# One instruction stream, two orders: attention and channel mixing with tables derived under a GpSimd and VectorE exclusion

## The chip, the cores and the metric

The kernel runs on one core of a Trainium2 chip. A core has engines that work side by side, each on its own list of instructions and in the order of that list: TensorE (PE in the profile; PEld is its loading of weights) multiplies matrices into PSUM, VectorE (DVE) and ScalarE (ACT) work element by element and over rows, GpSimd (POOL) does element-wise work from and to SBUF, and SyncE (SP) issues transfers. The metric is the device time of one execution in microseconds (us), lower is better.

## The reference

```
kv_pool = kv.reshape(B, H//4, 4, W//4, 4, C).mean(axis=(2, 4))     # 768 keys per batch
k = v = kv_pool.reshape(B, -1, C) @ w_sr
s = (q @ k.T) / sqrt(C);  s -= s.max(-1);  a = exp(s);  a /= a.sum(-1) + 1e-9
x = a @ v                                                          # 4 batches, 12288 rows, 128 channels
x_prev = x shifted down by one row (zero at the top)
xk = mu_k * x + (1 - mu_k) * x_prev;   xr = mu_r * x + (1 - mu_r) * x_prev
h = relu(xk @ w_k)**2                                              # 1024 hidden channels
out = sigmoid(xr @ w_r) * (h @ w_v)
```

## The kernel before

A tile is 512 rows of one batch, so there are 24 tiles a batch and 96 in all. The products run in 16-bit halves: an operand is split into a rounded part and a rest (a name that ends in `h` and one in `l`), and TensorE multiplies the pairs that matter. One tile goes through these steps; the name of a step in the tables stands first, the tile or buffer that the profile shows in brackets.

- `qf` loads the queries, `qh` (ACT) rounds them, `ql` (POOL) takes the rest.
- For each of 4 groups of 128 rows, s = 0 to 3: `S` (PE) the scores against 768 keys, `nm` (DVE) their negative maximum, `ex` (ACT) the exponential (`pe`; for the fourth group it is written back into `S`), `rc` (DVE) the reciprocal of the sums, `f1` (ACT) and `f2` (DVE) the two halves of the normalised weights (`pp<-pe` from SBUF, `pp<-S` from PSUM for the fourth group), `tt` (SP) their transposing transfer (`pT`).
- `AV0` to `AV5` (PE) the sums over the keys (`px`); `xek` and `xer` (ACT) scaled copies for the shift; `xk`, `xr` (DVE) the mixed rows; `xkh`, `xrh` (DVE) and `xkl`, `xrl` (POOL) their halves.
- For each of 4 pairs of hidden blocks, f = 0 to 3: `ha`, `hb` (PE, `ph`), `r` (ACT, `rr`) the positive part, `k2` the square in 32 bits (`kk`; DVE for f = 0 and 1, ACT for 2, and for 3 on DVE back into `ph`), `kh` its rounded half (ACT; DVE for f = 2), `kl` the rest (POOL; DVE for f = 3), `va`, `vb` (PE, `pv`) the second product.
- `z` (PE, `pz`), `E` and `th` (ACT), `E1`, `T1`, `g` (DVE) the gate, `o` (DVE) the output, `so` (SP) its store.

Beside the tiles, `batch_prep` prepares the keys of the next batch: `L_kv` and `br` load and pool them piece by piece over 12 tiles, `pk` and `ks` project them, `am` and `ex` find a scale, `ksh` (a 512-column and a 256-column piece), `kb`, `kd` make the score operands (`ksh`, `kbl`), `vh`, `vl` (`vv`) and `tv` (`vT`) the value operand, `dg`, `dm`, `xt`, `sv`, `uz` the constants of the gate. The weights are prepared once at the start (`w..._wk0` and the like).

What sets the order is a table. Every step is put into a heap under a number, and the heap is emptied from the smallest on; each engine keeps the order in which its instructions were given:

```
if i < len(EARLY):
    places, base = EARLY[i], 0.0
elif i >= NTILES - len(LATE):
    places, base = LATE[i - (NTILES - len(LATE))], i * PERIOD
else:
    places, base = WHEN, i * PERIOD
```

So the first 8 tiles have a table each (`EARLY`), the last 4 too (`LATE`), and the 84 between share one (`WHEN`), shifted by `PERIOD` = 19.3 a tile; `PREP` and `SUM` place the preparation of the next batch in the same way, `ONCE` the weights and the first batch's keys. The numbers only rank; no step waits for a clock. A buffer is taken from its ring when the step that fills it is given: three PSUM buffers serve `S` and `ph` in turn, one serves `px`, `pz` and `pk`, one `pv`. Thus the order also says which step must have read a buffer before another may fill it: `ha0` waits for the fourth `kl` of the tile ahead, `ha1` for the third `ex`, `ha2` for the fourth `f2`, `ha3` for `r2`, the first `S` for `k20`, the second for `k21`, the third for the first `ex`, the fourth for the second. All steps go through one helper, so that nearly all rows of the profile have its line, L39; they are told apart by the names of their tiles.

Of the kernel before, what the change touches and what calls it, by code (L numbers as in the profile page):

```python
# [73 lines left out]
def tile_kernel(ctx, tc, qT, kv0a, kv0b, kvw, head, w_k, w_v, w_r, outT):  # L74
# [712 lines left out]
    for i, (b, t) in enumerate(seq):  # L787
# [44 lines left out]
    "L": 45.13984, "br": 55.31514,  # L832
# [53 lines left out]
    },  # L886
    {
# [268 lines left out]
```

## Time and profile before

| | |
|---|---|
| median of 3 runs | 1902.59 us (1902.36 to 1903.91) |
| profiled execution | 1902.11 us, its span 1900.3 us |
| TensorE | 1844.3 us busy, 97% of the span, 8837 matmuls |
| VectorE | 1750.9 us, 92%, 2400 instructions |
| ScalarE | 1690.0 us, 89%, 2430 |
| GpSimd | 1110.4 us, 58%, 793 |

The busy time of TensorE is modelled (its matmuls are pipelined), so idle time in it says more than busy time. A row of a time line reads: start and length in us, engine, line, operation, what is written from what, its shape, and in brackets the idle time of the engine before it with what ended it. In a row by tiles the three numbers are the shortest, median and longest duration in ns.

### The profile page before, as it was taken

What the parts mean: (1) busy time and instruction counts of PE and PEld (TensorE: products, weight loads), DVE (VectorE), ACT (ScalarE), POOL (GpSimd) and SP (SyncE); (2) the same over time, 40 slices, a digit from 0 to 9 for tenths busy, and PEclk for the clock granted to TensorE, in tenths of its full rate; (3) what the DMA queues carried; (4) which work ended last, traced back from release to release, by engine and by line L of the source; (5) the groups of instructions that cost most, each with busy time, mean ns of one, the idle gap of its engine ahead of it and who ended that gap; (6) DMA issues with size and microseconds to landing.
All of it is one profiled execution on the core that took longest, in us unless ns stands there. A gap on an engine that the chain in (4) does not pass through costs nothing. (4 is left out here: it accounts for less than half of the span.)

```text
span 1900.3 us, 26528 instructions
## 1 busy us (share of the span) xinstructions
PE 1844.3 (97%) x8837; PEld 925.9 (49%) x8983; DVE 1750.9 (92%) x2400; ACT 1690.0 (89%) x2430; POOL 1110.4 (58%) x793
## 2 busy tenths in 40 slices
PE   6899999999999999999999999999999999999999
PEld 3344455445454545445555555544545454545454
DVE  8999999999999999999999999999998989899997
ACT  4788899889999999989999999988999999999997
POOL 2455566566556666556656666656655555555555
PEclk9999999999999999999999999999999999999999
DMA  7655655545465656455556665545645454545462
GB/s 231 136 117 129 147 137 120 106 107 124 99 145 130 148 131 146 96 113 117 119 113 140 139 138 140 130 97 110 120 107 117 107 116 108 115 109 108 91 126 56
DMA packets 643945, 232.12 MB, mean 122 GB/s; under 512 B 612320, under 2 KB 612576, under 8 KB 643808
## 3 DMA queue, kind: packets, MB, share of 16 engines
q1 hardware_dynamic: 643808, 230.43, 54.8%
q8 instruction: 70, 1.15, 0.2%
q14 instruction: 67, 0.55, 0.1%
HBM read 52.63 MB, written 25.17 MB: 41 GB/s over the span
## 5 line engine op out<-in xcount | busy, mean ns | idle before, releaser
L39 POOL TENSOR_TENSOR kl<-kk,kh 128x1024 bf16<-128x1024 f32 x288 | 685.3, 2380 | 182.4 <-ACT kh L39 119.9
L39 ACT ACTIVATE rr<-ph 128x1024 f32<-128x1024 f32 x384 | 392.0, 1021 | 19.3 <-PE ph L39 5.3
L39 PE MATMUL px<-pT,vT 128*128 128x512 f16 x1728 | 391.9, 379 | 2.3 <-DMA pT<-pp 2.2
L39 DVE TENSOR_REDUCE nm<-S 128x1 f32<-128x768 f32 x384 | 360.9, 952 | 27.5 <-PE S L39 22.1
L39 POOL TENSOR_TENSOR xkl<-xk,xkh 128x512 f16<-128x512 f32 x96 | 145.3, 1514 | 320.8 <-DVE xkh L39 318.1
L39 PE MATMUL ph<-xkh,wkl 128*128 128x512 f16 x768 | 293.2, 382 | 15.6 <-DVE pp L39 6.4
L39 ACT ACTIVATE kh<-rr 128x1024 f16<-128x1024 f32 x288 | 304.9, 1059 | 1.5 <-PE pv L39 0.7
L39 DVE SCALAR_TENSOR_TENSOR pp<-pe,rc,pp 128x768 f16<-128x768 f32 x288 | 300.3, 1045 | 0.0
L39 PE MATMUL ph<-xkh,wkh 128*128 128x512 f16 x768 | 292.4, 381 | 0.0
L39 PE MATMUL pv<-kh,wvl 128*128 128x512 f16 x768 | 292.0, 380 | 0.1
L39 PE MATMUL pv<-kh,wvh 128*128 128x512 f16 x768 | 291.1, 379 | 0.0
L39 ACT ACTIVATE pp<-pe,rc 128x768 f16<-128x768 f32 x288 | 267.7, 933 | 4.8 <-DVE rc L39 2.6
L39 ACT ACTIVATE pe<-S,nm 128x768 f32<-128x768 f32 x288 | 262.7, 912 | 8.7 <-DVE nm L39 8.7
L39 PE MATMUL S<-ksh,qh 128*128 128x512 f32 (+1 forms) x768 | 269.4, 432 | 0.0
L39 PEld LDWEIGHTS <-vT 128*128 128x128 f16 x1728 | 168.7, 98 | 206.1 <-issue 3.6
L39 PE MATMUL S<-kbl,qh 128*128 128x256 bf16 (+1 forms) x768 | 251.2, 327 | 2.7
L39 POOL TENSOR_TENSOR xrl<-xr,xrh 128x512 f16<-128x512 f32 x96 | 113.5, 1183 | 239.0 <-DVE xrh L39 239.0
L39 PEld LDWEIGHTS <-wkh 128*128 128x128 f16 x1536 | 150.6, 98 | 180.3 <-issue 12.6
L39 DVE TENSOR_TENSOR kk<-ph,rr 128x1024 f32<-128x1024 f32 x192 | 232.5, 1212 | 2.4 <-ACT rr L39 2.1
L39 PE MATMUL S<-kbl,ql 128*128 128x256 bf16 (+1 forms) x717 | 215.1, 325 | 14.3 <-DVE pp L39 5.3
L39 PE MATMUL ph<-xkl,wkh 128*128 128x512 f16 x768 | 228.2, 379 | 0.0
L39 PE MATMUL pv<-kl,wvb 128*128 128x512 bf16 x673 | 187.1, 379 | 4.7
(119 smaller groups left out, 2655.5 us busy)
## 6 DMA issues: line engine op xcount, KB each, us to landing
qf<-qT SPq DMA_DIRECT2D x96, 256.0 KB, 2.7
outT<-o SPq DMA_DIRECT2D x96, 256.0 KB, 2.7
kvt<-kvw SPq DMA_DIRECT2D x36, 512.0 KB, 3.7
pT<-pp SPq DMA_TRANSPOSE x384, 3.9
kva<-kv0a SPq DMA_DIRECT2D x8, 512.0 KB, 9.8
kvb<-kv0b SPq DMA_DIRECT2D x4, 512.0 KB, 6.4
land<-moe_w_k SPq DMA_DIRECT2D x2, 512.0 KB, 5.4
land<-moe_w_v SPq DMA_DIRECT2D x2, 512.0 KB, 9.7
```

The source lines that it names most:

```text
L39: return self.tc.keep_in_program_order(op(*args, **kwargs))
```

## The change

All numbers of the tables `WHEN`, `PREP`, `SUM`, `ONCE`, `EARLY` and `LATE` are others; the code, `PERIOD`, the rings and the split of the work over the engines are the same. The new tables were derived with a rule that the old ones did not have: a GpSimd step and a VectorE step that works in SBUF exclude each other, and whichever comes first is served first. The same instructions are given on each engine, in another order. Two lines of `WHEN` as a sample:

```
 WHEN = {
...
-    "tt0": 122.93608, "tt3": 123.31903, "f11": 123.34952,
...
+    "tt0": 133.32336, "xcr": 138.76318, "AV4": 140.17205,
...
 }
```

ScalarE, in a steady tile, from its third `f1` (`pp<-pe`) on. First before (`s_...` is a buffer of scales):

```order
L39 ACTIVATE pp<-pe,rc 128x768
L39 ACTIVATE kh<-rr 128x1024
L39 ACTIVATE xer<-px,s_4555 128x512
L39 ACTIVATE xek<-px,s_4555 128x512
L39 ACTIVATE rr<-ph 128x1024
L39 ACTIVATE pp<-pe,rc 128x768
L39 ACTIVATE kk<-rr 128x1024
L39 ACTIVATE pe,sm<-S,nm 128x768
L39 ACTIVATE rr<-ph 128x1024
L39 ACTIVATE pe,sm<-S,nm 128x768
L39 ACTIVATE kh<-rr 128x1024
L39 CAST qh<-qf 128x512
```

And now the same place:

```order
L39 ACTIVATE pp<-pe,rc 128x768
L39 ACTIVATE kh<-rr 128x1024
L39 ACTIVATE xek<-px,s_4662 128x512
L39 ACTIVATE xer<-px,s_4662 128x512
L39 ACTIVATE rr<-ph 128x1024
L39 ACTIVATE pp<-pe,rc 128x768
L39 ACTIVATE kk<-rr 128x1024
L39 ACTIVATE pe,sm<-S,nm 128x768
L39 ACTIVATE rr<-ph 128x1024
L39 CAST qh<-qf 128x512
L39 ACTIVATE kh<-rr 128x1024
L39 ACTIVATE pe,sm<-S,nm 128x768
```

`xek` and `xer` have changed places (on VectorE `xk` now comes ahead of `xr` too), and `qh` and the last `kh` stand ahead of the second `pe`.

VectorE, in the tiles in which the keys of the third batch are prepared. Before, the 256-column `ksh`, and two tiles later `vv`:

```order
L39 SCALAR_TENSOR_TENSOR pp<-pe,rc,pp 128x768
L39 TENSOR_SCALAR ex<-ex 128x1
L39 TENSOR_SCALAR exi<-ex 128x1
L39 TENSOR_SCALAR exs<-exi 128x1
L39 RECIPROCAL ivs<-exs 128x1
L39 CAST ksh<-ks 128x256
L39 SCALAR_TENSOR_TENSOR xr<-px,s_4555,xer 128x512
```

```order
L39 TENSOR_TENSOR o<-pv,E 128x512
L39 TENSOR_TENSOR kk<-ph,rr 128x1024
L39 SCALAR_TENSOR_TENSOR pp<-pe,rc,pp 128x768
L39 SCALAR_TENSOR_TENSOR vv<-ks,ivs,vv 128x768
L39 SCALAR_TENSOR_TENSOR pp<-S,rc,pp 128x768
L39 TENSOR_TENSOR kk<-ph,rr 128x1024
```

Now, `vv` and then the 256-column `ksh`, both in one tile:

```order
L39 CAST xrh<-xr 128x512
L39 CAST ksh<-ks 128x512
L39 TENSOR_TENSOR kk<-ph,rr 128x1024
L39 SCALAR_TENSOR_TENSOR pp<-pe,rc,pp 128x768
L39 SCALAR_TENSOR_TENSOR vv<-ks,ivs,vv 128x768
L39 SCALAR_TENSOR_TENSOR pp<-S,rc,pp 128x768
```

```order
L39 CAST kh<-kk 128x1024
L39 CAST xkh<-xk 128x512
L39 CAST ksh<-ks 128x256
L39 TENSOR_REDUCE nm<-S 128x1
L39 TENSOR_TENSOR ph<-ph,rr 128x1024
```

`ksh` (256) has moved from behind the reciprocal to right behind `xkh`; `vv` has kept its neighbours but for the 512-column `ksh`, which now stands in front of that group's `kk`, and `o`, which has left it.

VectorE, among the early tiles, behind the second tile's first two `kk`. Before:

```order
L39 TENSOR_TENSOR kk<-ph,rr 128x1024 x2
L39 TENSOR_SCALAR th<-th 128x512
L39 SCALAR_TENSOR_TENSOR pp<-pe,rc,pp 128x768
L39 TENSOR_REDUCE nm<-S 128x1
L39 SCALAR_TENSOR_TENSOR xk<-px,s_368,xek 128x512
L39 TENSOR_REDUCE nm<-S 128x1
L39 CAST xkh<-xk 128x512
L39 CAST kh<-kk 128x1024
L39 SCALAR_TENSOR_TENSOR E<-th,E 128x512
```

Now:

```order
L39 TENSOR_TENSOR kk<-ph,rr 128x1024
L39 SCALAR_TENSOR_TENSOR pp<-pe,rc,pp 128x768
L39 TENSOR_TENSOR kk<-ph,rr 128x1024
L39 SCALAR_TENSOR_TENSOR E<-th,E 128x512
L39 TENSOR_REDUCE nm<-S 128x1
L39 SCALAR_TENSOR_TENSOR xk<-px,s_452,xek 128x512
L39 TENSOR_REDUCE nm<-S 128x1
L39 SCALAR_TENSOR_TENSOR xr<-px,s_452,xer 128x512
L39 TENSOR_TENSOR o<-pv,E 128x512
L39 TENSOR_REDUCE nm<-S 128x1
```

The steps with both sources in SBUF (`pp<-pe`, `E<-th,E`) have moved to directly behind a `kk`, and a run of steps that read PSUM follows them.

More of the change, by code (lines that the diff above doesn't have):

```diff
@@ L804 @@
 WHEN = {
[17 rows of a table removed]
[7 rows of a table added]
+    "xck": 141.87398, "xek": 142.03537, "xer": 142.22498, "xk": 142.40427, "xr": 142.58396,
[9 rows of a table added]
 }
 PREP = {
[4 rows of a table removed]
[4 rows of a table added]
 }
 SUM = {
-    "L": 45.13984, "br": 55.31514,
+    "L": 65.37223, "br": 79.195,
 }
 ONCE = {
[29 rows of a table removed]
[28 rows of a table added]
 }
@@ L868 @@
     {
[17 rows of a table removed]
-    },
-    {
[17 rows of a table removed]
-    },
-    {
[7 rows of a table removed]
-        "AV4": 176.11741, "xck": 176.5236, "xek": 177.02373, "xk": 179.13729, "xkh": 180.45319,
[9 rows of a table removed]
-    },
-    {
[8 rows of a table removed]
-        "xk": 201.62598, "xkh": 208.34152, "ha1": 213.22611, "xkl": 213.60283, "xrh": 213.8469,
[8 rows of a table removed]
-    },
-    {
[17 rows of a table removed]
-    },
-    {
[8 rows of a table removed]
-        "xk": 241.50051, "xkh": 243.94708, "xrh": 244.1967, "ha0": 244.21385, "xkl": 244.3984,
[8 rows of a table removed]
-    },
-    {
[8 rows of a table removed]
-        "xk": 259.59986, "xrh": 262.28631, "xkh": 262.32977, "ha0": 266.61381, "xkl": 267.01243,
[8 rows of a table removed]
-    },
-    {
[7 rows of a table removed]
-        "AV5": 271.90604, "xcr": 274.05055, "xer": 275.94464, "xek": 276.91977, "xr": 277.15018,
[9 rows of a table removed]
[8 rows of a table added]
+        "xkh": 145.82771, "ha0": 147.73394, "xr": 148.19736, "xkl": 150.52983, "xrh": 150.54586,
[8 rows of a table added]
+    },
+    {
[7 rows of a table added]
+        "AV5": 159.69251, "xck": 160.80234, "xek": 162.49849, "xer": 165.39887, "xr": 167.58438,
[9 rows of a table added]
+    },
+    {
[7 rows of a table added]
+        "xek": 179.83256, "xcr": 181.30798, "xer": 181.83538, "xck": 183.13181, "xk": 183.29868,
[9 rows of a table added]
+    },
+    {
[7 rows of a table added]
+        "AV1": 199.98883, "xck": 200.01456, "xer": 200.05713, "xek": 200.06782, "xr": 201.1657,
+        "xk": 202.95953, "xrh": 205.85223, "xkh": 206.16685, "xkl": 207.6449, "xrl": 207.91575,
[8 rows of a table added]
+    },
+    {
[7 rows of a table added]
+        "AV1": 218.79166, "xer": 219.073, "xcr": 220.47205, "xek": 221.17581, "xr": 221.98162,
+        "xk": 223.76274, "xkh": 223.89597, "xkl": 226.46877, "xrh": 227.86795, "ha0": 230.011,
[8 rows of a table added]
+    },
+    {
[17 rows of a table added]
+    },
+    {
[17 rows of a table added]
+    },
+    {
[17 rows of a table added]
     },
@@ L1023 @@
     {
[7 rows of a table removed]
-        "xcr": 141.30178, "xck": 141.3035, "xer": 142.09219, "xr": 142.98018, "xk": 143.46442,
-        "xrh": 144.33588, "xkh": 147.25734, "xkl": 149.18043, "ha0": 150.61545, "hb0": 150.617,
[8 rows of a table removed]
-    },
-    {
[17 rows of a table removed]
-    },
-    {
[7 rows of a table removed]
-        "xer": 141.35008, "xek": 142.75073, "xcr": 143.52487, "xr": 146.04453, "xk": 147.30314,
-        "xkh": 147.54007, "xrh": 147.86579, "ha0": 148.28497, "ha1": 149.52576, "xkl": 150.11563,
[8 rows of a table removed]
-    },
-    {
[7 rows of a table removed]
-        "AV2": 140.74517, "xek": 140.75134, "xer": 140.98971, "xk": 143.82198, "xkh": 145.10936,
[9 rows of a table removed]
[7 rows of a table added]
+        "xck": 141.31546, "xer": 142.5985, "xr": 143.40341, "xek": 143.85939, "xk": 143.97965,
[9 rows of a table added]
+    },
+    {
[17 rows of a table added]
+    },
+    {
[17 rows of a table added]
+    },
+    {
[7 rows of a table added]
+        "AV0": 138.22219, "xek": 143.2128, "xer": 143.4251, "xk": 143.8168, "xkh": 145.06434,
[9 rows of a table added]
     },
```

487 rows, old and new, of tables (EARLY, LATE, ONCE, PREP) are left out of this document.

## The prediction

> **What bounds the kernel now.** I read the stretches of the span first, then the waits of TensorE, then the time lines around them. Columns of a stretch: its length, then busy microseconds and instructions of PE, PEld, DVE, ACT, POOL, the granted clock, the DMA share, GB/s.
>
> ```profile
> core 0: us, PE busy (x) PEld busy (x) DVE busy (x) ACT busy (x) POOL busy (x), PEclk, DMA share, GB/s
> 0.00:35.00 35.00, 21.29 (x60) 10.05 (x62) 26.87 (x65) 11.32 (x20) 7.18 (x11) 1.00 0.75 276
> 35.00:250.00 215.00, 194.37 (x915) 97.13 (x929) 209.05 (x289) 184.22 (x270) 111.24 (x85) 0.98 0.60 130
> 250.00:335.00 85.00, 84.63 (x410) 42.90 (x416) 78.91 (x105) 77.83 (x113) 51.90 (x34) 1.00 0.61 132
> 335.00:400.00 65.00, 61.66 (x300) 31.07 (x303) 59.83 (x84) 56.33 (x82) 37.32 (x26) 1.00 0.53 110
> 795.00:860.00 65.00, 61.66 (x300) 30.95 (x303) 59.82 (x84) 56.31 (x84) 37.11 (x26) 1.00 0.53 109
> 1255.00:1320.00 65.00, 61.66 (x299) 30.92 (x302) 59.82 (x84) 56.32 (x84) 37.07 (x26) 1.00 0.52 110
> 1800.00:1900.00 100.00, 94.48 (x444) 45.26 (x450) 87.45 (x107) 81.99 (x109) 57.76 (x38) 1.00 0.41 87
> ```
>
> In the steady stretch (250 to 335) PE is busy 84.63 of 85 us: nothing that moves on another engine can make it shorter, only longer. TensorE stands idle in three places: at the start (20.6 of the 215 us from 35 to 250), in the three stretches in which the next batch's keys are prepared (3.3 us each, three times alike), and in the last 100 us (5.5). From 35 to 250 VectorE is the busiest, 209.05 of 215. The waits say on whom TensorE stands: us in total, times, the longest; from 61 us (when the first tile's hidden layer is under way) to 250, then from 335 to 400.
>
> ```profile
> PE ph L39 <- DVE pp L39: 3.2, 2, 2.1
> PE S L39 <- DVE kk L39: 2.5, 2, 1.8
> PE S L39 <- ACT pe L39: 2.4, 1, 2.4
> PE ph L39 <- DVE kk L39: 1.2, 1, 1.2
> PE ph L39 <- DVE kl L39: 0.5, 1, 0.5
> ```
>
> ```profile
> PE ph L39 <- ACT rr L39: 2.0, 2, 1.1
> PE ph L39 <- DVE pp L39: 0.8, 1, 0.8
> PE S L39 <- ACT pe L39: 0.3, 1, 0.3
> ```
>
> So 9.8 us in the early part and 3.1 us in one preparation. The tiles show where they come from: shortest, median and longest ns.
>
> ```profile
> L39 DVE SCALAR_TENSOR_TENSOR pp<-pe,rc,pp x288: 997/1007/2894, 39.4 to 1864.0; 128x768 f16<-128x768 f32 x144
> L39 DVE SCALAR_TENSOR_TENSOR pp<-S,rc,pp x96: 1003/1008/1019, 41.2 to 1856.7; 128x768 f16<-128x768 f32 x96
> L39 DVE TENSOR_SCALAR rc<-sm x104: 154/169/2091, 35.8 to 1854.1; 128x4 f32<-128x4 f32 x88, 128x2 f32<-128x2 f32 x16
> L39 DVE SCALAR_TENSOR_TENSOR E<-th,E x96: 658/660/2495, 98.0 to 1895.8; 128x512 f32<-128x512 f32 x96
> L39 DVE TENSOR_TENSOR o<-pv,E x96: 673/683/693, 100.2 to 1896.5; 128x512 f32<-128x512 f32 x96
> ```
>
> The same step from PSUM (`pp<-S`) varies by 16 ns, from SBUF (`pp<-pe`) by 1.9 us. An excess of about 1.9 us is that of a step that began just behind a GpSimd product, as here:
>
> ```profile
> 91.74 2.19 POOL L39 TENSOR_TENSOR kl<-kk,kh 128x1024 bf16<-128x1024 f32 x1 [3.29 <-DVE kk L39]
> 91.85 2.89 DVE L39 SCALAR_TENSOR_TENSOR pp<-pe,rc,pp 128x768 f16<-128x768 f32 x1
> ```
>
> Begun 0.11 us behind `kl`, `pp` ends 0.81 us behind it: it stood still until `kl` was over and then took its 1.0 us. The Trainium skill, "SBUF — State Buffer", section "SBUF: two separate sides", has this as an exclusive lock: whoever starts first keeps the shared port pair for the whole instruction, a Vector instruction with two SBUF inputs or in a 2-port mode being one that asks for it, one with a PSUM source not; the rows above agree.
>
> **The change, term by term.** No instruction is added or removed; all ranks move.
>
> *Preparation of the keys.* Before, `ksh` (256 columns) and `vv` come behind a GpSimd product:
>
> ```profile
> 808.60 2.49 POOL L39 TENSOR_TENSOR kl<-kk,kh 128x1024 bf16<-128x1024 f32 x1 [0.49 <-ACT kh L39]
> 809.65 1.58 DVE L39 CAST ksh<-ks 128x256 fp32r<-128x256 f32 x1
> 810.26 0.27 PE L39 MATMUL S<-kbl,ql 128*128 128x256 bf16 x1
> 811.16 0.74 DVE L39 SCALAR_TENSOR_TENSOR xr<-px,s,xer 128x512 f32<-128x512 f32 x1
> 811.26 0.28 PE L39 MATMUL S<-kbl,ql 128*128 128x256 bf16 x1
> 811.93 0.69 ACT L39 ACTIVATE xek<-px,s 128x512 f32<-128x512 f32 x1 [2.83 <-DVE xr L39]
> 813.58 0.38 PE L39 MATMUL ph<-xkh,wkl 128*128 128x512 f16 x1 [1.14 <-ACT rr L39]
> ```
>
> ```profile
> 845.67 2.18 POOL L39 TENSOR_TENSOR kl<-kk,kh 128x1024 bf16<-128x1024 f32 x1 [1.22 <-ACT kh L39]
> 845.79 2.89 DVE L39 SCALAR_TENSOR_TENSOR vv<-ks,ivs,vv 128x768 f16<-128x768 f32 x1
> 849.66 0.39 PE L39 MATMUL ph<-xkh,wkl 128*128 128x512 f16 x1 [0.77 <-DVE pp L39]
> ```
>
> The held `ksh` makes `xr` late, `xr` makes ScalarE's `xek` late (2.83 us idle), behind `xek` stands `rr`, and TensorE waits for `rr`. The held `vv` does the same through `pp`. In the new order `ksh` (256) follows `xkh` at once, a place that before is often that of `kh`:
>
> ```profile
> 97.39 0.68 DVE L39 CAST kh<-kk 128x1024 f16<-128x1024 f32 x1
> 97.54 1.53 POOL L39 TENSOR_TENSOR xkl<-xk,xkh 128x512 f16<-128x512 f32 x1 [2.76 <-DVE xkh L39]
> ```
>
> VectorE's next instruction is 0.15 us ahead of the `xkl` that the same `xkh` releases, and has its 0.68 us undisturbed while `xkl` is the one that grows. So `ksh` gets in first; `xkl` waits some tenths, which `hb0`, far behind on TensorE, hides. `vv` now stands behind the first `pp` of the period, ahead of the point where ScalarE has made the `kh` that lets `kl` start; the 512-column `ksh` stands right behind `xrh`. The second cause goes too: ScalarE's wait inside the `xer`, `xek` pair.
>
> ```profile
> ACT xek L39 <- DVE xr L39: 110.5, 85, 3.9
> ```
>
> Before, `xek` waits for `xr`, 110.5 / 85 = 1.3 us a tile, and `rr` of the third pair stands behind it. Now `xek` and `xer` stand next to each other and `xr` comes after both. Walking one period of the new order by these rows (TensorE back to back, each engine's rows in turn) I find every step of the preparation done before TensorE asks. What is late next would be `vv` if VectorE came about 0.5 us later: it would then fall behind `kl` again. Term: 3 x 3.1 = 9.3 us saved; bounds 0 and 10 (3 x 3.3).
>
> *Early tiles (61 to 250).* The held steps there are those behind `kl`, `xkl`, `ql`. In the new order the pattern is turned: where before `th`, `pp` (from SBUF) and later `E` stood in GpSimd's way behind two `kk`, the new rows put `pp` and `E` directly behind a `kk`, ahead of GpSimd's start, and then six steps with a PSUM source, under which two `kl` of about 2.2 us can run. If all went, 9.8 us. But the new order keeps pairs that contend (`xrl` ahead of `th`, `kl` ahead of the next `pp`), and VectorE's own work in this stretch stays at 209 less the held time. With `pp`, `rc` and `E` alone holding up to 1.9 us a time, I take half of the 9.8: 5 us saved; bounds 9.8 saved and 4 lost (two new waits of the longest size seen, 2.1).
>
> *Filling (up to 61).* Ahead of the first `xkh` two `nm` (0.95 us each by the page's group, quoted below) leave VectorE's list and one weight step of 512 columns, between 0 and the 1.0 us of a `pp`, enters it: 0.9 to 1.9 us earlier. The loads are in another order, of the same bytes. I take 1 us saved; bounds 3 saved, 2 lost. The clock of 0.98 from 35 to 250 is about 4 us of slow TensorE behind idle stretches; I count no gain there and let it widen the range by 2.
>
> *Steady tiles.* Nothing, as long as no loop of waits is longer than TensorE's own rows. The period is (1896.5 - 100.2) / 95 = 18.9 us by the `o` row. The tightest loop of the new order, by which it could go wrong, is the rival below; it comes to 17.7.
>
> *End.* After TensorE's last row come one `o` and its transfer, as before. Zero; bounds 1.5 either way.
>
> Sum: 9.3 + 5 + 1 = 15.3. The profiled execution took 1902.1 (1900.3 span, 1.8 around it), 0.5 below the median of the runs. 1902.6 - 15.3 = 1887.
>
> **The rivals.** *Everything goes* (9.3 + 9.8 + 3 + 1.5 = 23.6): 1879. For it: the held steps are behind nearly all of the 9.8. Against: VectorE has 6 us of idle in that stretch at most.
>
> *Only the preparation gains*: the early part keeps its 9.8 with the waits at other steps: 1893. For it: VectorE stays the bound there, and its work is the same.
>
> *It doesn't do what it says*: the exclusion is there but its waits only change place, as TensorE, 97% busy, has the same rows: 1902, within 0.2% (3.8 us, about what a measurement of this kernel can tell). The Trainium skill, "Perfetto Trace Analysis", section "Identifying the Most-Contended Engine", would have one work on the engine with the highest occupancy first; read so, an order that leaves TensorE's rows alone changes nothing. The first table speaks against it: the idle time is 20.6 + 3 x 3.3 in four known places.
>
> *Slower: the loop through ScalarE.* The new order puts `qh` and one `kh` ahead of the second `pe`, which frees the PSUM buffer for the fourth `S`. The loop: `S` (1.0 us, from 810.26 to 811.26), `nm`, the fourth exponential, all of ScalarE's next period up to the second `pe`, then `S` again.
>
> ```profile
> L39 DVE TENSOR_REDUCE nm<-S 128x1 f32<-128x768 f32 x384 | 360.9, 952 | 27.5 <-PE S L39 22.1
> L39 ACT ACTIVATE E<-pz,uz 128x512 f32<-128x512 f32 x96 | 68.2, 711 | 1.0 <-PE pz L39 1.0
> L39 ACT ACTIVATE th<-pz,uz 128x512 f32<-128x512 f32 x96 | 68.0, 708 | 0.1
> L39 ACT ACTIVATE pe<-S,nm 128x768 f32<-128x768 f32 x288 | 262.7, 912 | 8.7 <-DVE nm L39 8.7
> ```
>
> ScalarE is busy 77.83 of 85, so 17.3 us of a period. Of these `E`, `th` and the third `pe` (0.7 + 0.7 + 0.9, less some 0.2 by which neighbours overlap) lie off the loop: 15.2. With `S` 1.0, `nm` 0.95 and about 0.5 for four handovers: 17.7, so 1.2 below 18.9. If the loop came out above 18.9, each tenth would cost 0.1 x 88 steady tiles = 9 us; it outweighs the 15.3 from 0.17 on, so from a misjudgement of 1.4 us. At 0.3: 1902.6 + 26 - 15 = 1914.
>
> **How the numbers follow.** The forecast (preparation and half of the early part) 0.49, everything 0.10, only the preparation 0.20, no change 0.12, slower 0.09. Faster by over 0.2% (below 1898.8) holds the first three, 0.79; the same 0.12; slower 0.09. The likeliest alone gives 1887, with 1882 to 1893 of its own (the early part from all to nothing). The range from 1877 (everything, and 2 for the clock) to 1903 (no change) leaves out the slower case and a tenth for the ends.
>
> **What would show it.** Right: from 335 to 400 and in its two likes PE busy at about 64.7 of 65; `ksh` (256) at some 0.3 us and `vv` at 1.0 in the later batches; ScalarE's wait of `xek` for `xr` gone from the waits; the longest `pp`, `rc`, `E` well below 2 us; the early waits of TensorE at about 5. Wrong: a wait that repeats once per tile on TensorE in the steady stretch (`S` for `pe` above all), or `vv` still at 2.9 us, or new waits of 1 to 2 us before 250.

## The result: 24.5 us faster

| | before | changed |
|---|---|---|
| median | 1902.6 us (1902.36 to 1903.91) | 1878.1 us (1876.5 to 1878.7) |
| profiled execution, its span | 1902.1, 1900.3 | 1878.4, 1876.7 |
| ratio | | 0.9869 (95% interval 0.9851 to 0.9886) |

The forecast was 1887, the range 1877 to 1903. The time came out near the low end, where the rival "everything goes" stood (1879). These are the stretches of the changed kernel, with the columns of the prediction:

```profile
35.00:250.00 215.00, 204.69 (x992) 103.09 (x991) 203.21 (x298) 193.85 (x284) 115.32 (x88) 0.98 0.67 138
250.00:335.00 85.00, 85.00 (x415) 42.49 (x413) 79.61 (x112) 77.33 (x112) 46.16 (x37) 1.00 0.58 124
335.00:400.00 65.00, 65.00 (x322) 32.67 (x320) 60.65 (x88) 60.57 (x87) 38.48 (x28) 1.00 0.66 123
795.00:860.00 65.00, 65.00 (x323) 32.92 (x322) 60.80 (x87) 60.57 (x88) 39.02 (x30) 1.00 0.62 118
1255.00:1320.00 65.00, 65.00 (x322) 32.75 (x321) 60.09 (x88) 59.92 (x88) 39.05 (x31) 1.00 0.57 115
```

TensorE has no idle time left in the three preparations, and 10.3 us instead of 20.6 between 35 and 250. From 61 to 250 us these are all of its waits, and from 250 to 1780 us it has none:

```profile
PE ph L39 <- ACT pe L39: 2.7, 1, 2.7
PE px L39 <- issue: 0.3, 1, 0.3
```

For a sum the span is divided at rows that both kernels have: the first matmul of the first `ha0` (60.1 us before, 61.0 now), the `o` of the ninth tile (247.8, 239.4) and of the 89th (1779.2, 1759.5). The first fence is before, the second the changed kernel:

```profile
60.10:247.80 187.70, 177.01 (x835) 87.58 (x850) 182.03 (x241) 160.84 (x230) 103.11 (x76) 0.98 0.58 128
247.80:1779.20 1531.40, 1515.69 (x7334) 764.17 (x7453) 1410.64 (x1920) 1395.23 (x2010) 923.04 (x652) 1.00 0.55 120
1779.20:1900.30 121.10, 115.18 (x544) 55.61 (x552) 106.55 (x133) 101.44 (x136) 70.34 (x47) 1.00 0.41 87
```

```profile
61.00:239.40 178.40, 178.13 (x863) 88.39 (x863) 169.43 (x245) 164.68 (x235) 101.78 (x77) 0.99 0.62 133
239.40:1759.50 1520.10, 1520.09 (x7453) 763.26 (x7451) 1398.90 (x1920) 1397.67 (x2009) 865.89 (x653) 1.00 0.59 121
1759.50:1876.70 117.20, 112.19 (x540) 54.23 (x538) 99.19 (x130) 98.16 (x133) 66.01 (x46) 1.00 0.43 90
```

- Up to the first `ha0`: 0.9 later.
- Early part: 9.3 shorter, although 13 more weight loads, and so 13 more matmuls, lie in it (863 instead of 850). At 0.204 us each (1520.1 us for 7451 of them in the middle) that is some 2.7 us of work, so the same work takes about 12 us less. TensorE's idle time accounts for 10.4 of it (10.7 to 0.3). The rest goes with the clock. Before, 0.51 was granted from 60.4 to 63.8 us and 0.50 from 97.9 to 101.3; in the changed kernel there is one such stretch, 0.50 from 61.9 to 65.3. One stretch less is 3.4 x 0.5 = 1.7 us.
- Steady tiles with the three preparations: 11.3 less (by the two `o` rows 11.2).
- End: 3.9 shorter, with 14 weight loads less in it (2.9 us of work), so 1.0 less for the same work; idle time 5.9 to 5.0.

Together 0.9 - 9.3 - 11.3 - 3.9 = -23.6, the difference of the spans. (That the early part holds more work and the end less is due to `o`, which has another place relative to TensorE in the new order.) Idle time read from the rows of before is a little too long: its trace has 8837 matmuls for 8983 weight loads, and where a record is missing the row shows TensorE idle for 0.05 us. The waits hold no such gaps.

The steps that were held before, by tiles:

```profile
L39 DVE SCALAR_TENSOR_TENSOR vv<-ks,ivs,vv x4: 1007/1012/1012, 35.1 to 1284.8; 128x768 f16<-128x768 f32 x4
L39 DVE CAST ksh<-ks x8: 283/352/427, 28.8 to 1293.4; 128x512 fp32r<-128x512 f32 x4, 128x256 fp32r<-128x256 f32 x4
L39 DVE TENSOR_SCALAR rc<-sm x104: 146/163/374, 38.2 to 1831.0; 128x4 f32<-128x4 f32 x88, 128x2 f32<-128x2 f32 x16
L39 DVE SCALAR_TENSOR_TENSOR E<-th,E x96: 660/691/694, 88.5 to 1872.2; 128x512 f32<-128x512 f32 x96
L39 DVE SCALAR_TENSOR_TENSOR pp<-pe,rc,pp x288: 1001/1008/2787, 40.1 to 1842.5; 128x768 f16<-128x768 f32 x144
```

`vv` was 2.89 us in the later batches and is 1.01; the longest `rc` fell from 2.09 to 0.37, the longest `E` from 2.50 to 0.69. One `pp` of 2.79 us is left, at 1837 us in the end. Over the span VectorE is busy 1716.3 us instead of 1750.9 with the same 2400 instructions. `ksh` and `vv` now get in ahead of GpSimd, as the prediction placed them, `ksh` by 0.16 us and `vv` by 0.47:

```profile
836.62 0.42 DVE L39 CAST xkh<-xk 128x512 f16<-128x512 f32 x1
836.96 0.28 DVE L39 CAST ksh<-ks 128x256 fp32r<-128x256 f32 x1
837.12 1.16 POOL L39 TENSOR_TENSOR xkl<-xk,xkh 128x512 f16<-128x512 f32 x1 [2.12 <-DVE xkh L39]
828.39 1.01 DVE L39 SCALAR_TENSOR_TENSOR vv<-ks,ivs,vv 128x768 f16<-128x768 f32 x1
828.86 2.54 POOL L39 TENSOR_TENSOR kl<-kk,kh 128x1024 bf16<-128x1024 f32 x1 [1.46 <-ACT kh L39]
```

### The profile page after: what moved, and what is told of

Same layout as the page of the kernel before. It is cut to its first block, busy times and chain, and to the rows that moved or that the text cites. A ratio compares the mean times of both kernels' runs of the same rounds, so it can differ in the third digit from the quotient of the medians.

```text
span 1876.7 us, 26777 instructions
## 1 busy us (share of the span) xinstructions
PE 1849.2 (99%) x8983; PEld 925.4 (49%) x8983; DVE 1716.3 (91%) x2400; ACT 1692.3 (90%) x2430; POOL 1047.1 (56%) x793
## 4 chain that ended last, share of the span: by engine, by line
PE 96%; DVE 2%; DMA 1%; ACT 1%; issue 0%; SPq 0%; DVEq 0%; ACTq 0%
PE ph L39 26%; PE pv L39 26%; PE S L39 20%; PE px L39 20%; PE pz L39 3%; PE pk L39 1%; DVE nm L39 0%; DMA kva<-kv0a 0%; DVE pp L39 0%; DMA kvb<-kv0b 0%; ACT rr L39 0%; DVE kl L39 0%; DVE ph L39 0%; ACT kh L39 0%; DVE top L39 0%
## 5 line engine op out<-in xcount | busy, mean ns | idle before, releaser
L39 POOL TENSOR_TENSOR kl<-kk,kh 128x1024 bf16<-128x1024 f32 x288 | 665.5, 2312 | 236.6 <-ACT kh L39 185.3
L39 ACT ACTIVATE rr<-ph 128x1024 f32<-128x1024 f32 x384 | 392.5, 1023 | 62.1 <-PE ph L39 49.7
L39 DVE TENSOR_REDUCE nm<-S 128x1 f32<-128x768 f32 x384 | 364.8, 952 | 70.6 <-PE S L39 70.1
L39 DVE SCALAR_TENSOR_TENSOR pp<-pe,rc,pp 128x768 f16<-128x768 f32 x288 | 292.6, 1018 | 1.9 <-ACT pp L39 1.9
L39 ACT ACTIVATE pe<-S,nm 128x768 f32<-128x768 f32 x288 | 258.8, 899 | 6.3 <-DVE nm L39 5.8
L39 POOL TENSOR_TENSOR xkl<-xk,xkh 128x512 f16<-128x512 f32 x96 | 113.4, 1181 | 261.1 <-DVE xkh L39 261.1
L39 PE MATMUL S<-kbl,ql 128*128 128x256 bf16 (+1 forms) x768 | 231.6, 328 | 8.4 <-ACT pe L39 3.9
L39 PE MATMUL pv<-kl,wvb 128*128 128x512 bf16 x768 | 213.1, 379 | 0.0
```

The costliest lines, as they stand in the source:

```text
L39: return self.tc.keep_in_program_order(op(*args, **kwargs))
```

## The experiments

"Held" is what a VectorE step takes beyond the shortest of its shape. The last four columns are us: the start of the first `ha0`, from there to the ninth tile's `o`, on to the 89th tile's `o`, and the rest of the span. The first of them scatters from run to run: the six kernels with the start tables of the changed one as they are (changed, e2, e4, e9, e10, e11) have 60.5 to 63.8, the six with those of before 59.3 to 61.6.

| kernel | median, us | against before (95%) | first `ha0` | early | middle | end |
|---|---|---|---|---|---|---|
| before | 1902.6 | | 60.1 | 187.7 | 1531.4 | 121.1 |
| changed | 1878.1 | 0.9869 (0.9851 to 0.9886) | 61.0 | 178.4 | 1520.2 | 117.2 |
| e1 steady tables | 1910.3 | 1.0042 (1.0028 to 1.0055) | 60.5 | 203.6 | 1520.3 | 124.0 |
| e2 start tables | 1908.1 | 1.0027 (1.0016 to 1.0039) | 63.8 | 192.6 | 1531.2 | 120.9 |
| e3 before, half `kl` | 1890.3 | 0.9934 (0.9921 to 0.9946) | 61.6 | 181.6 | 1525.5 | 120.3 |
| e4 changed, half `kl` | 1877.3 | 0.9866 (0.9852 to 0.9879) | 60.5 | 178.5 | 1520.2 | 115.9 |
| e5 pair | 1893.1 | 0.9948 (0.9935 to 0.9962) | 59.9 | 187.4 | 1522.3 | 120.4 |
| e6 two steps | 1893.9 | 0.9952 (0.9939 to 0.9964) | 61.1 | 187.9 | 1521.9 | 121.1 |
| e7 before, quarter products | 1878.7 | 0.9874 (0.9861 to 0.9888) | 59.3 | 175.2 | 1522.3 | 119.8 |
| e8 changed, three moves | 1874.8 | 0.9854 (0.9841 to 0.9868) | 59.9 | 178.0 | 1520.2 | 116.5 |
| e9 changed, two steps undone | 1885.2 | 0.9908 (0.9893 to 0.9923) | 62.0 | 178.1 | 1525.2 | 117.2 |
| e10 changed, long hold | 1891.7 | 0.9941 (0.9926 to 0.9956) | 63.1 | 177.6 | 1532.3 | 117.3 |
| e11 changed, short | 1877.9 | 0.9871 (0.9854 to 0.9887) | 62.0 | 177.1 | 1520.2 | 117.1 |

### One part of the tables at a time (e1, e2)

```
e1: before, with WHEN, PREP, SUM of the changed kernel
e2: before, with ONCE, EARLY of the changed kernel
```

> The order of before, with only the tables of the 84 steady tiles and of the key preparation (WHEN, PREP, SUM) taken from the changed kernel. Theory H (TensorE's idle time is handed on by VectorE steps held behind a GpSimd product): the three preparations lose their idle time, 11 us less than before (10 to 12.5), 1891 to 1892; from 335 to 400 us TensorE busy over 64.7 of 65; the start keeps its idle time of 20 us between 35 and 250. Theory S (the gain of the parts hangs together, since the eighth tile's order has to fit the ninth's): new waits of 2 to 4 us around the ninth tile, and less than 8 us gained.

> The order of before, with only the tables of the weights and first keys and of the first 8 tiles (ONCE, EARLY) taken from the changed kernel. Theory H: 11.5 us less than before (10 to 13), 1890 to 1892: TensorE idle about 10 us between 35 and 250 instead of 20.6; the three preparations keep their 3.3 us each. Both parts together give the whole of 23.7 but for about 1 us of the end. Theory S: a part alone gives less than 8 us, and the two don't add up.

Both came out slower than before, by 7 and 5 us, so theory H misses both times; yet each holds a clean part. In e1 the middle is 1520.3 us, the whole 11.2 of the changed kernel, and TensorE has no wait from 250 to 1780 us; in e2 the middle is unchanged. New waits stand where tiles of one order meet tiles of the other. From 61 to 250 us TensorE waits in e1 (the first three of seven rows), and in e2 (the first of seven):

```profile
PE S L39 <- ACT pe L39: 7.0, 3, 2.5
PE ph L39 <- DVE pp L39: 3.8, 3, 2.3
PE ph L39 <- ACT pe L39: 2.5, 2, 1.5
```

```profile
PE ph L39 <- DVE kl L39: 7.4, 6, 2.6
```

In e1 9.3 us of waits lie between 180 us and the ninth tile's `o` (1.2 before), in e2 9.6 between 170 us and that row (none in the changed kernel). The early part takes 203.6 us in e1 and 192.6 in e2, instead of 187.7; e1 loses another 3 us at its end. Some of this is the clock: from 35 to 250 us 0.96 was granted in e1 and 0.95 in e2, against 0.98 before, and 0.03 of 215 us is 6 us. Theory S holds for the seam, and larger than it said; theory H for the middle of e1. What the early part gains by itself can't be told from these two, and e3 and e7 were made for it.

### The order of before with shorter GpSimd products (e3, e4, e7)

```
e3, e4 (f = 0, 1, 2; the product reads the half twice):
-  out=new(f"kl{f}"), in0=st[f"kk{f}"], in1=st[f"kh{f}"]
+  out=new(f"kl{f}")[:, 0:T], in0=st[f"kk{f}"][:, 0:T], in1=st[f"kh{f}"][:, 0:T]
e7: 0:T // 4 in the same places, and for ql, xkl, xrl
-  out=new(f"x{x}l"), in0=st[f"x{x}"], in1=st[f"x{x}h"]
+  out=new(f"x{x}l")[:, 0:P], in0=st[f"x{x}"][:, 0:P], in1=st[f"x{x}h"][:, 0:P]
```

> The order of before; GpSimd's kl covers only the first 512 of its 1024 columns, and the second product uses these twice (3 of the 4 hidden pairs), so TensorE's work is the same and a VectorE step that begins just behind a kl is held by 1.1 us at most instead of 2.1. Theory H (holds): the longest pp and vv fall from 2.9 to 1.9 us or less, the time of held VectorE steps falls from 41 to about 20 us, and the time by 7 to 15 us, to 1887 to 1896. Theory O (the idle time comes from the sequence of VectorE's and ScalarE's own work, held or not): 1899 to 1903, within 3 us of before.

> The changed kernel with the same half kl as in the run before. Theory H: nothing is held there, so nothing is gained: within 2 us of the changed kernel, 24 us (22 to 26) less than before. Theory O: the shorter kl brings the same in both orders.

> The order of before, with all of GpSimd's products of the tiles cut to a quarter (kl to 256 of 1024 columns for 3 of 4 pairs, xkl, xrl and ql to 128 of 512, which TensorE then reads four times over): its work is the same, and nothing holds a VectorE step for more than about 0.6 us. Theory H: the early part, the preparations and the end lose their idle time without any new order: 1879 to 1885, 18 to 24 us less than before. Theory O (the half kl had what is to be had, 12.9; the rest of the early idle time comes from the sequence): 1887 to 1891.

No step is moved here, and in e7 TensorE reads the quarter four times. With half a `kl` the order of before gains 12.9 us, the changed order about 1. These are the longest `pp` and `vv` in e3, and what TensorE still waits for from 335 to 400 us there (3.1 us before, 1.3 now):

```profile
L39 DVE SCALAR_TENSOR_TENSOR pp<-pe,rc,pp x288: 998/1007/2024, 40.9 to 1851.8; 128x768 f16<-128x768 f32 x144
L39 DVE SCALAR_TENSOR_TENSOR vv<-ks,ivs,vv x4: 1007/1911/1914, 38.4 to 1296.3; 128x768 f16<-128x768 f32 x4
```

```profile
PE ph L39 <- ACT rr L39: 1.0, 2, 0.8
PE S L39 <- ACT pe L39: 0.3, 1, 0.3
```

The early part of e3 is 6.1 us shorter than before, but TensorE still stands idle for 7.1 us of it (10.7 before); the rest of that gain goes with the clock, 1.00 instead of 0.98. So e3 settles the preparation more than the early part. With a quarter the order of before takes 1878.7 us, as the changed kernel does. These are the longest `pp` and `E` in e7, and all of TensorE's waits from 61 to 250 us (9.8 before):

```profile
L39 DVE SCALAR_TENSOR_TENSOR pp<-pe,rc,pp x288: 998/1007/1205, 39.4 to 1838.8; 128x768 f16<-128x768 f32 x144
L39 DVE SCALAR_TENSOR_TENSOR E<-th,E x96: 658/660/912, 91.6 to 1872.2; 128x512 f32<-128x512 f32 x96
```

```profile
PE S L39 <- DVE kk L39: 0.7, 1, 0.7
PE S L39 <- ACT pe L39: 0.5, 1, 0.5
PE ph L39 <- DVE pp L39: 0.2, 1, 0.2
```

The early part goes from 187.7 to 175.2 us, the middle from 1531.4 to 1522.3, the end from 121.1 to 119.8: without long holds the old order gains nearly all that the change brought, in the middle 9.1 of 11.2. Theory H holds; O, which left the rest of the early idle time to the sequence, falls. Two things stay mixed. The clock of the early part rose as well, from 0.98 to 1.00; but 8.4 us of waits are gone whatever the clock is worth. And shorter products are also finished earlier. Apart from one of 1.5 us at 30 us, neither TensorE, VectorE nor ScalarE waits for a GpSimd product in the trace of before, which speaks against that as the cause; it wasn't tried apart. The Trainium skill, "SBUF — State Buffer", section "SBUF: two separate sides", says that the loser is blocked for the other's whole instruction and doesn't share; the longest `pp` of 2.89, 2.02 and 1.21 us for `kl` of about 2.2, 1.2 and 0.5 us agrees.

### The preparation: two ways to take the stall out of the old order (e5, e6)

```
 WHEN (e5)                                PREP (e6)
-"xr": 141.80224, "xek": 142.28626        -"ksh1": 83.51417, "vl": 121.214
+"xek": 141.80224, "xr": 142.28626        +"ksh1": 89.63,    "vl": 124.3
```

> The order of before, with one pair of ranks exchanged in the steady table: xek now ranks ahead of xr, so that ScalarE's two scaled copies stand in front of both VectorE steps that read px. No engine's list changes but for one place at the seam to the early tiles; what goes is that ScalarE's xek has to wait for VectorE's xr (1.3 us a tile). Theory C (two causes: the held ksh reaches TensorE only through xr, xek, rr): the wait of ph for rr, 2.0 us in each preparation, goes although ksh is still held for 1.3 us; 5 to 7 us less, 1896 to 1898; the wait for pp (0.8) stays. Theory H alone (the held step itself costs the time, by whatever way): rr or another step stays late, 1901 to 1903.

> The order of before, with two steps moved in the key preparation alone: the 256-column ksh right behind xkh, and vv behind xk, where GpSimd stands idle in the steady tile of before. The wait of xek for xr stays. Theory H: both are held no more (0.3 and 1.0 us long), the three preparations lose most of their idle time: 8 to 11 us less, 1892 to 1895. Rival (the VectorE work itself is what is late, since vv's 1.0 us now stands ahead of two nm and xkh): half or less of that, 1897 to 1901.

e5 exchanges two numbers and gains 9.0 us. `ksh` (the first row) and `vv`, 2.89 us, are held as long as before; from 335 to 400 us only the wait for `pp` is left, with TensorE busy 64.22 of 65:

```profile
L39 DVE CAST ksh<-ks x8: 274/592/1586, 27.9 to 1312.4; 128x256 fp32r<-128x256 f32 x4, 128x512 fp32r<-128x512 f32 x4
```

```profile
PE ph L39 <- DVE pp L39: 0.8, 1, 0.8
```

ScalarE's wait of `xek` for `xr`, 110.5 us before, is 3.9 us there, once. e6 leaves that wait and takes the holds away, and gains 8.1; TensorE is busy 64.90 of 65. In its rows the three later `ksh` of 256 columns take 0.28 to 0.29 us; the 0.72 is a 512-column one:

```profile
L39 DVE SCALAR_TENSOR_TENSOR vv<-ks,ivs,vv x4: 1009/1009/1010, 37.9 to 1304.5; 128x768 f16<-128x768 f32 x4
L39 DVE CAST ksh<-ks x8: 275/418/721, 27.4 to 1313.1; 128x256 fp32r<-128x256 f32 x4, 128x512 fp32r<-128x512 f32 x4
```

The middle is 9.1 us shorter in e5 and 9.5 in e6. Together that is 18.6, where only 11.2 are to be had: the stall needs both causes, a late VectorE and a ScalarE that waits for it, and taking away either one takes most of it. Theory C holds, with more than it said; its rival and that of e6 (VectorE's plain work) fall.

### Holds put back into the changed order (e9, e10, e11)

```
 PREP (e9)                                WHEN
-"vl": 120.37969, "ksh1": 128.57933       -"f22": 122.92745
+"vl": 120.83,    "ksh1": 123.2           +"f22": 123.2  (e10)   +"f22": 123.3  (e11)
```

> The changed kernel, with two steps of the key preparation put where GpSimd's kl holds them again: vv behind the pp that reads PSUM, the 256-column ksh between xk and xr. Theory C (in the new order ScalarE's xek no longer waits behind VectorE, so a hold must eat VectorE's own slack before TensorE sees it): vv 2.5 to 2.9 us and ksh 1.0 to 1.8 us long, but only 0 to 1 us of TensorE's time per preparation: 0 to 3 us more than the changed kernel, 1878 to 1881. Theory H alone (each held microsecond costs one): 3 us per preparation, 1886 to 1888.

> The changed kernel, with the third pp of every steady tile (f22) moved from directly behind the second kk to behind xk, so that kl starts ahead of it and holds it. By the steady tile of the changed kernel xk then stands idle for 0.8 us for ScalarE's xer, and pp is held for about 0.7 us more: xr and the nm behind it come 1.6 us later, while VectorE has 0.95 us of idle time in a tile. Theory H (a hold is paid from the point where VectorE's slack is used up): the pp 1.6 to 1.9 us long, and 0.4 to 0.7 us per tile in 84 tiles: 34 to 59 us more than the changed kernel, 1912 to 1937. Rival (a tile's length is set by TensorE and the delay is taken up by the buffers): 1878 to 1884.

> As the run before, but with pp one step later, behind xr, where kl is over when it starts: the same steps have moved, the idle 0.8 us for xer is there, the hold is not (pp 1.0 to 1.2 us). Theory H: 0 to 0.2 us per tile, 0 to 17 us more than the changed kernel, 1878 to 1895, and clearly less than the run before. Rival (it is the later place of pp and its transfer, not the hold): as slow as the run before or slower.

In e9 the two steps are 1.5 and 1.3 us longer again, and from 335 to 400 us TensorE waits:

```profile
373.65 2.48 DVE L39 SCALAR_TENSOR_TENSOR vv<-ks,ivs,vv 128x768 f16<-128x768 f32 x1
379.38 1.56 DVE L39 CAST ksh<-ks 128x256 fp32r<-128x256 f32 x1
```

```profile
PE S L39 <- ACT pe L39: 1.0, 2, 0.7
PE pz L39 <- DVE xr L39: 0.2, 1, 0.2
```

The middle is 5.1 us longer, 1.7 per preparation, for 2.8 held; the median is 7 above the changed kernel's, of which the rest is not in the middle and within the scatter of the start. Theory C expected at most 1 per preparation and misses, H alone expected 3 and overshoots: in the new order about six tenths of a hold are paid, no longer through `rr` but through a late `nm`, `pe` and the `S` that waits for its buffer. These are links of the loop which the prediction had as its slower rival, but it is VectorE that starts it: ScalarE stands idle for 2.84 us there until `nm` is done, so its own rows are not what closes the loop.

e10 and e11 differ by one place of one step. The same place of a steady tile, e10 and then e11:

```profile
569.67 0.75 DVE L39 SCALAR_TENSOR_TENSOR xk<-px,s,xek 128x512 f32<-128x512 f32 x1 [0.85 <-ACT xer L39]
570.34 1.61 DVE L39 SCALAR_TENSOR_TENSOR pp<-pe,rc,pp 128x768 f16<-128x768 f32 x1
571.88 0.74 DVE L39 SCALAR_TENSOR_TENSOR xr<-px,s,xer 128x512 f32<-128x512 f32 x1
```

```profile
565.54 0.75 DVE L39 SCALAR_TENSOR_TENSOR xk<-px,s,xek 128x512 f32<-128x512 f32 x1 [0.85 <-ACT xer L39]
566.21 0.74 DVE L39 SCALAR_TENSOR_TENSOR xr<-px,s,xer 128x512 f32<-128x512 f32 x1
566.87 1.01 DVE L39 SCALAR_TENSOR_TENSOR pp<-pe,rc,pp 128x768 f16<-128x768 f32 x1
```

Both wait 0.85 us for `xer`; only e10's `pp` is held, by 0.6 us here and by 0.8 in most tiles like it. e11 is as fast as the changed kernel, e10 is 14 us slower, 12.1 in the middle. So it is the hold that costs, not the later place of `pp`. The size was overestimated (34 to 59). A tile takes 19.28 instead of 18.95 us, but only while VectorE also pools the next batch's keys (`br`, 1.2 us a tile). In the middle these are 26 tiles, some 8 us; the rest lies in the tiles of the preparations. In the last batch, without `br`, the tile stays at 18.95; but there `xk` waits 1.6 us for `xer`, `pp` starts that much later behind `kl`, takes 1.10 us and is hardly held. So e10 shows that about four tenths of such a hold are paid where VectorE is full, and not what a hold costs where VectorE has time to spare. For that there is the kernel before: an `rc` at 402.6 us takes 1.09 us, of which 0.9 are a hold, and TensorE has no wait from 400 to 795 us.

### A version faster than both (e8)

```
 EARLY[2]   -"ex0": 142.74657, "nm1": 145.86997     LATE[0]   -"o": 181.53863
            +"ex0": 142.4339,  "nm1": 145.05                  +"o": 180.9
```

> The changed kernel with three ranks moved, at its two longest late waits of TensorE: in the third tile ex0 ahead of the first tile's xek and nm1 ahead of the first tile's xk, which fills 2.3 us in which VectorE stands idle and frees the PSUM buffer of the first ha0 earlier (2.7 us of wait); near the end the output step of the 93rd tile ahead of a pp that is held by GpSimd for 1.8 us (1.1 us of wait). Theory: TensorE has no other wait behind these, so what is saved there stays saved: 3 to 4 us less than the changed kernel, 1874 to 1875. Rival: the first ha0 then waits for xkh instead, and the steps behind it for xkl: 0.5 to 2 us less, 1876 to 1877.5.

This takes 1874.8 us. The first `ha0` now waits 0.7 us for `xkh` where it waited 2.7 for the PSUM buffer, but 1.0 us of that older wait is back right behind it, as the only wait from 61 to 250 us. Near the end `pz` waits 0.5 where `pv` waited 1.1:

```profile
PE ph L39 <- DVE xkh L39: 0.7, 1, 0.7
```

```profile
PE pz L39 <- DVE xk L39: 0.5, 1, 0.5
```

By medians it is 3.3 us below the changed kernel, by spans 2.1; the intervals of the two ratios overlap, so against the changed kernel this is likely, not shown. The time is that of the theory, the new waits are those of the rival.

## Why the prediction was right, and where its sizes were off

What a wait costs comes first, as the prediction took it to be the idle time shown. A matmul is shown with 0.38 us, while the next one starts 0.22 us after it when nothing is in the way:

```profile
133.80 0.38 PE L39 MATMUL ph<-xkh,wkl 128*128 128x512 f16 x1 [2.11 <-DVE pp L39]
134.02 0.38 PE L39 MATMUL ph<-xkh,wkh 128*128 128x512 f16 x1
```

So the idle time before a late matmul is counted from 0.16 us after the place where it could have started, and a wait costs 0.16 us more than it shows.

- **Preparation of the keys** (9.3, bounds 0 to 10): 11.2, beyond its upper bound. The two held steps were the cause, as argued (e6, e7); the price was too low. The three preparations have 12 waits that show 9.2 us in all, and 9.2 + 12 x 0.16 = 11.1. (The same working gives the 1.7 of e9: three waits, 1.2 us shown, and 0.5.) No stall lay outside the three stretches: the 84.63 of 85 us ahead of them was full, with 410 matmul records for 416 weight loads. That the pair `xer`, `xek` was "the second cause" was an understatement: it is by itself worth 9.1 (e5).
- **Early tiles** (5 of 9.8, bounds 9.8 and -4): about 12, of which 10.4 idle time. This is the term that was off by most, and the main reason why the forecast was 9 us too high. The step that failed is "I take half", and under it the argument against "everything goes": "VectorE has 6 us of idle in that stretch at most". That counted the held time as VectorE's work. With the holds gone the early part needs 169.4 us of VectorE instead of 182.0, by the rows above, for 245 instead of 241 instructions, and there is room for all of it. That "the new order keeps pairs that contend" was true of the list but hardly of the run: from 61 to 250 us four steps were longer than the shortest of their shape by over 0.1 us, 0.6 at most.
- **The clock** (no gain counted, 2 either way): one stretch of 3.4 us at half clock less in the early part, 1.7 us. Whether it is worth that isn't shown: e6, with the early tables of before, was granted 0.99 instead of 0.98 there, and its early part is not shorter (187.9 us against 187.7): TensorE stands idle for longer instead.
- **Filling** (1, bounds 3 and -2): 0.9 later. The six kernels with the new start tables reach the first `ha0` at 62.1 us on the mean, the six with the old ones at 60.4, so the sign was rather wrong, though the two overlap. The new order has a wait of 2.7 us of its own there, of which e8 leaves 1.7.
- **Steady tiles and end** (0): 18.95 us a tile as before, and about 1 less at the end.
- **The rivals.** "Everything goes", given 0.10, is what came. That its sum of 23.6 is the difference of the spans to the tenth is luck: 3 of it were to come from filling and 1.5 from the end, where 0.9 were lost and about 1 gained. The ScalarE loop did not close: TensorE has no wait from 250 to 1780 us. How large its room is wasn't measured; e9 and e10 reach TensorE through its links `nm`, `pe` and `S`, but from VectorE. "No change" fell with the first table.
- **What was to be seen**: PE at 64.7 or more, `ksh` 0.28, `vv` 1.01, `xek` no longer waiting for `xr`: right. Early waits of about 5: they are 3.0. Longest `pp` well below 2 us: wrong by the one at the end.

## What to carry to other kernels

An engine that stands at a lock is shown as busy, so a stretch at 97% may have room: compare the shortest and longest duration of each shape first, and take the difference off before arguing that the engine is full. A hold can cost nothing (`rc` at 402.6 us before), four to six tenths of its length (e10, e9) or about all of it (e6: 3 x 3.2 us of holds gone, 9.5 us gained in the middle), so look for it where side work (here `br`, `ksh`, `vv`) fills the engine. A stall can need two causes (e5, e6), and the cheaper one to remove can be a wait that has no data behind it (two ranks, 9 us). Half of one order and half of another, on the other hand, may fit badly where they meet (e1, e2).

## What the hardware showed that was not expected

A step of two columns is held like a long one: `rc`, 128x2, took 0.15 us at its shortest and 2.09 us behind a GpSimd product (at 146.3 us, 0.17 us behind the start of a `kl` of 2.23). GpSimd is held in turn: the median `xkl` took 1.54 us before and 1.16 in the new order, and GpSimd's busy time fell from 1110.4 to 1047.1 us with the same 793 instructions.

The clock of TensorE falls in pieces. Before, 0.50 was granted from 97.9 to 101.3 us, right behind a wait of 2.4 us, and 1.00 from there to 250, although a wait of 2.1 us lies at 133.8. The changed kernel has one such piece behind its wait of 2.7 us at 61.0, and e7, with 1.5 us of idle time between the first `ha0` and the ninth tile's `o`, has none there. What decides that a wait is followed by such a piece isn't shown here.
